# The next batch's scores in float32 ahead of time, q and k in joint tiles, and a softmax in three units of the plan

## The chip, the core and the metric

One core of one Trainium2 chip runs the whole program. The metric is the time on the device of one execution in microseconds, as the median of several. Engines are named as the profile names them: PE is TensorE, PEld its weight loads, DVE is VectorE, ACT is ScalarE, POOL is GpSimd, SP the queue that issues every DMA of this kernel.

## What is computed

For each of four batches with q, k and v of 6080 tokens by 256 channels, attention runs over channels, and a gated two-layer network follows (weights 256 by 2048 and 2048 by 256):

```
qn = q / (norm(q, axis=tokens) + 1e-6);  kn likewise
s  = kn.T @ qn / tau                      # 256 x 256 for each batch
a  = softmax(s, last axis)
x  = v @ a                                # tokens x 256
h  = x @ w_in                             # tokens x 2048
out = (h * sigmoid(1.702 h)) @ w_out      # tokens x 256
```

The weights arrive as float64 and are made float32 on the chip from their 32-bit words.

## The kernel before

**Work.** For each batch the 256 x 256 matrix `a` is folded into `w_in` (`weights`, 12 matmuls of 256 columns for each of 8 `p`), so that the long part goes from v straight to h. The tokens go in six chunks a batch (five of 1024, one of 960). For each chunk and each `p` (two blocks of 128 hidden columns) `unit` makes h with a scheme of seven products in place of eight (L753; each product is three matmuls, high by high, high by low and low by high, in float32r, whose three sums stand for float32), gates it on ACT, splits the result into `gh` and `gl`, and adds 24 matmuls into four output banks (L819). So there are 4 x 6 x 8 = 192 units of 45 matmuls of 512 (or 480) columns.

**Scores.** `s` needs the sum over all tokens of k.T q, and the norms need the sums of squares. The first batch has nothing to hide behind: its 47 tiles of 128 tokens and a tail of 64 are loaded at the start, and each tile's scores are two matmuls in plain float32 (`direct`, L497), into bank `psO0`. For batches 1 to 3, `rows` does it during the batch before, two units of two tiles at a time: load q and k, square them (ACT) and add up (DVE), split both into high and low parts (`qs`, `ks`), six float32r matmuls for each tile (L503) into a `psX` bank, and a DVE addition of that bank into `s_sum`. `finish` then makes norms, softmax and the transposed `a` (`aT_h`, `aT_l`) as one run of steps, in which both exponentials and a first gate (which fetches the gate's table back) are one entry.

**Order.** The program is written out ahead of time by `Plan`: each step has an engine, a modelled cost and a due time; the plan takes, whenever an engine is free, the ready step with the lowest due time, and the engines then run exactly that order. `DUE` holds due times within a unit, in which one unit is 45. Buffers are named slots; a step that uses a slot waits for all users of the slot's previous tenant. SP issues DMAs in the planned order too, and an issue that waits for its buffer holds all issues behind it.

**The first chunk** also converts the weights: in four groups `win_words` and `wout_words` bring words in, `to_float32` (one ACT and six DVE instructions) makes float32 of them, and `win_parts`, `wout_convert` split them. The matmuls on constants of `keep_warm` (8 at the start, 18 after the first scores) compute nothing that is used.

Of the kernel before, what the change touches and what calls it, by code (L numbers as in the profile page):

```python
# [172 lines left out]
def dve_fast(n):  # L173
# [15 lines left out]
def channel_attention_then_glu(  # L189
# [50 lines left out]


# [16 lines left out]
    def load(dst, src, kb, deps=(), uses=(), due=0.0):  # L258
        return g.add("SP", 50 + kb * 2.6, lambda: nc.sync.dma_start(dst(), src), deps, uses, due, lag=2200)
# [34 lines left out]
    def win_words(grp, c, due, slot, after=()):  # L294
        raw = sbuf(slot, [P, GW, 2], U32, "words")
        src = w_in[c * P : (c + 1) * P, 2 * grp * GW : 2 * (grp + 1) * GW].rearrange("p (f w) -> p f w", w=2)
        return raw, load(lambda: raw(), src, 512, after, [raw], due)

    def wout_words(u, due, slot, after=()):
        raw = sbuf(slot, [P, 2, C, 2], U32, "words")  # L300
        src = w_out[2 * u * P : 2 * (u + 1) * P, :].rearrange("(f p) (d w) -> p f d w", p=P, w=2)
        return raw, load(lambda: raw(), src, 512, after, [raw], due)

    def to_float32(out, lows, raw, ready, due, flat):

        n = GW
        lo = sbuf(lows, [P, n], U32, "low")

        def words(i):
            r = raw()  # L310
            return (r.rearrange("p f d w -> p (f d) w") if flat else r)[:, :, i]

        a = g.add(
            "ACT", act(n),
            lambda: nc.scalar.activation(out().bitcast(F32), words(1).bitcast(F32), AF.Abs),
            [ready], [raw, out], due,
# [17 lines left out]
                out().bitcast(U32), in0=words(1), scalar=0xC0000000, in1=out().bitcast(U32),  # L334
# [12 lines left out]
                lo().bitcast(F32), in0=words(0), scalar=2.0**-52, in1=lo().bitcast(F32),  # L347
# [4 lines left out]
        return tt(lambda: out(), lambda: out(), lambda: lo().bitcast(F32), ALU.add, n, [f], [out, lo], due + 6)  # L352

    win_ready = {}

    def win_convert(grp, c, words, due, lows):

        raw, ready = words
        wf = sbuf(f"t{2 * c}", [P, GW], F32, "wf")
        n = to_float32(wf, lows, raw, ready, due, False)  # L360
        store = g.add(
            "SP", 50 + 256 * 2.6,
            lambda: nc.sync.dma_start(win_f[c, :, grp * GW : (grp + 1) * GW], wf()),
            [n], [wf], due + 8, lag=2200,
        )
        win_ready[grp, c] = store
        return wf, n
# [3 lines left out]
    def wout_convert(u, words, due):  # L371
        raw, ready = words
        t = sbuf("t4", [P, GW], F32, "tf")
        n = to_float32(t, "t5", raw, ready, due, True)
        fs = slice(2 * u, 2 * u + 2)
        flat = lambda w: w[:, fs, :].rearrange("p f d -> p (f d)")
        h = cast(lambda: flat(wo_h), lambda: t(), GW, [n], [t], due + 7)
        l = low(lambda: flat(wo_l), lambda: t(), lambda: flat(wo_h), GW, [h], [t], due + 8)
        for f in (2 * u, 2 * u + 1):
            wo_ready[f] = l  # L380
# [3 lines left out]
    class Attention:  # L384
        def __init__(self, b):
            self.b = b
            self.stored = {}
            self.direct = b == 0
            self.units = [(t, min(UT, T - t), P) for t in range(0, T, UT)]
            if TAIL:  # L390
                self.units.append((T, 1, TAIL))
            self.S = bank("psO0", "s") if self.direct else sbuf("sa", [P, NC2 * C], F32, "s_sum")
            self.acc = [sbuf(f"t{6 + i}", [P, UT, C], F32, n) for i, n in enumerate(("acc_q", "acc_k"))]
            self.acc_n = [[], []]
            self.last = None
            self.raw = {}

        def body(self, src):
            return src[self.b, : T * P, :].rearrange("(p t) c -> p t c", p=P)

        def load_direct(self, t0, room, slot, due):

            nt = min(room, T - t0)
            for src, tag in ((q, "q"), (k, "k")):
                t = sbuf(RAW[tag][slot], [P, RT, C], F32, "raw_" + "qk"[tag == "k"])
                cuts = range(nt + 1) if t0 == 0 else (0, nt)
                ns = []
                for a, z in zip(cuts, cuts[1:]):
                    ns.append(load(
                        lambda a=a, z=z, t=t: t()[:, a:z, :], self.body(src)[:, t0 + a : t0 + z, :],  # L410
                        128 * (z - a), (), [t], due,
                    ))
                for o in range(nt):
                    self.raw.setdefault(t0 + o, []).append((t, o, ns[o] if len(ns) > 1 else ns[0]))
                if nt < room and TAIL:
                    n = load(lambda t=t: t()[:TAIL, nt, :], src[self.b, T * P :, :], 64, (), [t], due)
                    self.raw.setdefault(T, []).append((t, nt, n))

        def load_unit(self, u, due, after=()):
            t0, nt, pp = self.units[u]  # L420
            for src, tag in ((q, "raw_q"), (k, "raw_k")):
                t = sbuf(f"t{(u % 2) * 2 + (tag == 'raw_k')}", [P, UT, C], F32, tag)
                if pp == P:
                    n = load(lambda t=t: t()[:, :nt, :], self.body(src)[:, t0 : t0 + nt, :], 128 * nt, after, [t], due)
                else:
                    n = load(lambda t=t: t()[:pp, 0, :], src[self.b, T * P :, :], 64, after, [t], due)
                for o in range(nt):
                    self.raw.setdefault(t0 + o, []).append((t, o, n))

        def rows(self, us, due, after):  # L430

            S = turning("s")
            for i, u in enumerate(us):
                self.unit(u, due + 25 * i, after, S, due + 25 * len(us), i == 0, u == us[-1])
            sa = self.S
            src = lambda: S()[:, : NC2 * C]
            if us[0] == 0:
                self.last = g.add(
                    "DVE", dve(NC2 * C), lambda: nc.vector.tensor_copy(sa(), src()), [self.last], [S, sa],
                    due + 25 * len(us) + 20,  # L440
                )
            else:
                self.last = tt(
                    lambda: sa(), src, lambda: sa(), ALU.add, NC2 * C, [self.last], [S, sa], due + 25 * len(us) + 20,
                )

        def unit(self, u, due, after=(), S=None, pe_due=None, first_=True, last_=True):
            t0, nt, pp = self.units[u]
            S = S or self.S
            if t0 not in self.raw:  # L450
                self.load_unit(u, due - 30, after)
            w = nt * C
            ops = []
            for i, nm in enumerate(("q", "k")):
                buf, o, _ = self.raw[t0][i]
                ready = [self.raw[t0 + j][i][2] for j in range(nt)]
                src = lambda buf=buf, o=o: buf()[:pp, o : o + nt, :]
                acc = self.acc[i]
                if u == 0:
                    self.acc_n[i] = [g.add(  # L460
                        "ACT", act(w), lambda acc=acc, src=src: nc.scalar.activation(acc(), src(), AF.Square),
                        ready, [buf, acc], due + 2,
                    )]
                else:
                    sq = sbuf(f"t{4 + i}", [P, UT, C], F32, "sq")
                    s = g.add(
                        "ACT", act(w),
                        lambda sq=sq, src=src: nc.scalar.activation(sq()[:pp, :nt, :], src(), AF.Square),
                        ready, [buf, sq], due + 4,
                    )  # L470
                    a = lambda acc=acc: acc()[:pp, :nt, :]
                    self.acc_n[i].append(tt(
                        a, a, lambda sq=sq: sq()[:pp, :nt, :], ALU.add, w,
                        [s, self.acc_n[i][-1]], [sq, acc], due + 6,
                    ))
                if self.direct:
                    ops.append((buf, o, ready))
                    continue
# [34 lines left out]
        def finish(self, due):  # L513
# [70 lines left out]
            def fn_ee():  # L584
                for i in range(NC2):
                    fn_e(i)
# [377 lines left out]
```

## Time and profile before

| | |
|---|---|
| median of 3 runs | 2209.85 us (2207.35 to 2214.0) |
| the profiled execution | 2208.2 us, its span 2206.4 us |
| PE busy | 2170.5 us, 98% of the span |
| DVE busy | 1554.9 us, 70% |
| ACT busy | 1336.9 us, 61% |
| mean granted PE clock | 0.994 of full speed |
| moved by DMA | 316.33 MB, mean 143 GB/s |

Busy is time in which an engine has an instruction in work. A PE matmul is pipelined, so the rows' mean for one (about 390 ns) is longer than the step from one to the next. "Idle before" is what an engine stood still ahead of a group, and after the arrow what ended that. The granted clock (PEclk) is a share of 2.4 GHz, with 0.5 as the lower of its two levels.

### The profile page before, as it was taken

Reading aid. Unit: us, or ns where it says so; the run is one execution under the profiler, and the core shown is the slowest. Engines: PE = TensorE matmul, PEld = TensorE weight load, DVE = VectorE, ACT = ScalarE, POOL = GpSimd, SP = SyncE. Lnnn points to the kernel's source line nnn. Section 1 sums busy time; section 2 is a strip of 40 time slices with the busy share of each in tenths; the row PEclk is TensorE's granted clock in tenths of the full one; section 3 lists DMA queues with packets and bytes.
Section 4 is the critical chain, followed back from the end, with each engine's and each line's share of the span. In section 5 each row is a group of like instructions: output and inputs, shape, how many; then the busy total and the mean of one; then the engine's idle time right before and its main releaser. Section 6 shows DMA issues by size and latency. Waiting matters only on the chain.

```text
span 2206.4 us, 27182 instructions
## 1 busy us (share of the span) xinstructions
PE 2170.5 (98%) x10196; PEld 1825.0 (83%) x10196; DVE 1554.9 (70%) x2288; ACT 1336.9 (61%) x2126; POOL 4.9 (0%) x10
## 2 busy tenths in 40 slices
PE   9699999999999999999999999999999999999999
PEld 8578888888888888888888888888888888888887
DVE  7998687776776767766667677776676565565554
ACT  6567666665666666665666666665566555555553
POOL 0000000000000000000000000000000000000000
PEclk9799999999999999999999999999999999999999
DMA  8445344333553433423454343343355332333231
GB/s 293 134 166 189 114 170 160 136 106 122 208 204 115 152 139 141 160 101 121 167 190 179 115 162 134 121 157 118 114 190 191 115 130 103 120 122 113 108 105 49
DMA packets 78163, 316.33 MB, mean 143 GB/s; under 512 B 8400, under 2 KB 10448, under 8 KB 78032
## 3 DMA queue, kind: packets, MB, share of 16 engines
q1 hardware_dynamic: 78032, 314.61, 40.3%
q8 instruction: 80, 1.31, 0.2%
q14 instruction: 51, 0.42, 0.1%
HBM read 258.21 MB, written 56.36 MB: 143 GB/s over the span
## 4 chain that ended last, share of the span: by engine, by line
PE 90%; DVE 4%; DMA 3%; ACT 1%; issue 0%; SPq 0%; ACTq 0%
PE ps_o L819 45%; PE ps_X L753 23%; PE ps_Y L753 11%; PE ps_Z L753 6%; PE ps_s L503 5%; PE ps_w L657 1%; DMA w_ops<-w_op 1%; DMA wf<-win_f 1%; DMA v_raw<-in_vT 1%; DVE gl L273 0%; DVE acc_k L268 0%; DVE h L268 0%; DVE low L346 0%; DVE acc_q L268 0%; DMA raw_k<-in_k 0%
## 5 line engine op out<-in xcount | busy, mean ns | idle before, releaser
L753 PE MATMUL ps_X<-v_op,w_op 128*128 128x512 f32 (+1 forms) x2304 | 637.0, 390 | 12.1 <-ACT s L262 8.4
L819 PE MATMUL ps_o<-gh,wo_h 128*128 128x512 f32 (+1 forms) x1536 | 597.5, 389 | 0.5 <-DVE gh L265 0.5
L819 PE MATMUL ps_o<-gl,wo_h 128*128 128x512 f32 (+1 forms) x1536 | 596.1, 388 | 0.5 <-DVE gl L273 0.5
L819 PE MATMUL ps_o<-gh,wo_l 128*128 128x512 f32 (+1 forms) x1536 | 596.5, 388 | 0.0
L273 DVE TENSOR_TENSOR gl<-h,gh 128x1024 fp32r<-128x1024 f32 (+1 forms) x384 | 466.0, 1214 | 176.9 <-ACT gh L262 156.4
L753 PEld LDWEIGHTS ps_X<-v_op,w_op 128*128 128x128 f32 x2304 | 429.3, 188 | 104.6 <-ACT s L262 12.2
L262 ACT COPY s<-ps_X 128x512 f32<-128x512 f32 (+1 forms) x384 | 222.6, 580 | 314.0 <-PE ps_X L753 260.3
L769 ACT ACTIVATE h<-h 128x512 f32<-128x512 f32 (+3 forms) x384 | 318.8, 839 | 100.3 <-DVE h L268 93.0
L819 PEld LDWEIGHTS ps_o<-gl,wo_h 128*128 128x128 f32 x1536 | 288.5, 188 | 59.1 <-DVE gl L273 1.3
L819 PEld LDWEIGHTS ps_o<-gh,wo_h 128*128 128x128 f32 x1536 | 288.8, 188 | 55.0 <-DVE gh L265 0.9
L819 PEld LDWEIGHTS ps_o<-gh,wo_l 128*128 128x128 f32 x1536 | 288.9, 188 | 53.6
L753 PE MATMUL ps_Y<-v_op,w_op 128*128 128x512 f32 (+1 forms) x1152 | 323.5, 389 | 0.0
L753 PEld LDWEIGHTS ps_Y<-v_op,w_op 128*128 128x128 f32 x1152 | 215.7, 189 | 44.1 <-DVE h L268 1.9
L268 DVE TENSOR_TENSOR h<-ps_Y,s 128x512 f32<-128x512 f32 (+1 forms) x192 | 131.3, 684 | 137.1 <-ACT s L262 135.8
L262 ACT COPY u<-ps_X 128x512 f32<-128x512 f32 (+1 forms) x192 | 111.8, 583 | 187.7 <-PE ps_X L753 180.5
L262 ACT CAST gh<-h 128x1024 fp32r<-128x1024 f32 (+1 forms) x192 | 199.5, 1039 | 17.9 <-PE ps_o L819 13.0
L268 DVE TENSOR_TENSOR h<-ps_Z,s 128x512 f32<-128x512 f32 (+1 forms) x192 | 131.1, 683 | 89.9 <-ACT s L262 80.8
L265 DVE CAST gh<-h 128x1024 fp32r<-128x1024 f32 (+1 forms) x192 | 131.5, 685 | 59.2 <-PE ps_o L819 57.7
L268 DVE TENSOR_TENSOR h<-ps_Y,u 128x512 f32<-128x512 f32 (+1 forms) x192 | 131.4, 684 | 56.7 <-PE ps_Y L753 51.5
L753 PE MATMUL ps_Z<-v_op,w_op 128*128 128x512 f32 (+1 forms) x576 | 162.3, 390 | 0.0
L769 ACT ACTIVATE h<-ps_X 128x512 f32<-128x512 f32 (+1 forms) x192 | 113.8, 593 | 78.9 <-PE ps_X L753 72.3
L753 PEld LDWEIGHTS ps_Z<-v_op,w_op 128*128 128x128 f32 x576 | 109.0, 189 | 22.2
(98 smaller groups left out, 1606.1 us busy)
## 6 DMA issues: line engine op xcount, KB each, us to landing
w_op<-w_ops SPq DMA_DIRECT2D x184, 896.0 KB, 4.6
w_ops<-w_op SPq DMA_DIRECT2D x32, 896.0 KB, 4.6
v_raw<-in_vT SPq DMA_DIRECT2D x20, 1024.0 KB, 7.6
out_T<-osb SPq DMA_DIRECT2D x40, 512.0 KB, 3.2
raw_q<-in_q SPq DMA_DIRECT2D x69, 256.0 KB, 5.2
raw_k<-in_k SPq DMA_DIRECT2D x69, 256.0 KB, 5.3
wf<-win_f SPq DMA_DIRECT2D x24, 256.0 KB, 5.8
raw_q<-in_q SPq DMA_DIRECT2D x11, 512.0 KB, 6.9
```

Source lines behind the costliest of these rows:

```text
L262: return g.add("ACT", act(n, psum), lambda: nc.scalar.copy(dst(), src()), deps, uses, due)
L265: return g.add("DVE", dve_fast(n), lambda: nc.vector.tensor_copy(dst(), src()), deps, uses, due)
L268: return g.add("DVE", dve(n), lambda: nc.vector.tensor_tensor(dst(), a(), b(), op=op), deps, uses, due)
L273: lambda: nc.vector.tensor_tensor(dst(), src(), hi().bitcast(F32), op=ALU.subtract),
L503: nc.tensor.matmul(out, lhsT=rk()[:pp, j, l, ci], rhs=rq()[:pp, j, r, :], start=begin and m == 0, stop=last and m == 2, skip_group_check=True,
L657: nc.tensor.matmul(pb()[:, i * W2 : (i + 1) * W2], lhsT=l()[:, j, ci], rhs=r()[:, j, a * W2 : (a + 1) * W2], start=i == 0 and n == 0, stop ...
L753: nc.tensor.matmul(of(into), lhsT=wt()[:, m, l, :], rhs=v[m]()[:, r, :hw], start=begin and n == 0, stop=True, skip_group_check=True,)
L769: "ACT", act(n, psum), lambda: nc.scalar.activation(dst(), src(), AF.Gelu_apprx_sigmoid),
L819: nc.tensor.matmul(of(ob), lhsT=l[:, f, ds], rhs=rr()[:, n * hw : (n + 1) * hw], start=begin and i == 0 and m == 0, stop=end and i == 1 an ...
```

## The change

- **Joint tiles.** q and k of a unit lie in one tile of two times two times 256 elements; squares, their additions and the high and low splits take 1024 columns in one instruction instead of 512 twice. The weights' conversion takes 1024 columns at a time too, with one words buffer (`os`) and group 0's w_in words in v's buffer (`vr`). The first batch's loads come in units of two tiles through ten buffers, its tail second.
- **Scores ahead (`fill`).** The first 10 units (20 tiles) of the second batch are loaded behind the first batch's, and scored in plain float32 into bank `psO1`; 10 more are loaded and scored in the same way, two units in each of the first five units of the first chunk, through buffers of the next chunk's v. A DVE step (`gather`) adds each bank's sum into `s_sum`: six of them. `rows` later loads these units again for the squares alone and leaves out their splits and matmuls.
- **Softmax in three.** `finish` becomes `norms`, `spread` and `softmax`, with due times of their own; in steady state they belong to three successive units of the loop. Inside `softmax` the two halves of 128 rows go separately: each has its own exponential, reciprocal and transposes. For the first batch all three have the lowest due times. The 18 `keep_warm` matmuls go.
- **Smaller edits.** `between` takes the `psX` bank that the unit before doesn't use, without turning. In the first chunk the second cast to `gh` moves from DVE to ACT. The outputs share one buffer `os`. All due times are set anew, and the plan assumes 3200 ns for a DMA instead of 2200.

The core of the diff:

```diff
 DUE = {
-    "m1": -4, "s1": 5, "m2": 4, "m6": 31, "u2": -17, "c11": 13, "g11": 21, "m5": 35, "u4": 28,
-    "m7": 35, "c22": 5, "m3": 14, "g12": 2, "m4": 42, "c21": 30, "g2": 50, "h1": 60, "l1": 19,
-    "h2": 72, "l2": 37, "o": 137,
+    "m1": 2, "s1": -29, "m2": 6, "m6": 28, "u2": -46, "c11": 11, "g11": 50, "m5": 33, "u4": 20,
+    "m7": 25, "c22": 0, "m3": 9, "g12": 21, "m4": 49, "c21": -6, "g2": 56, "h1": 53, "l1": 53,
+    "h2": 52, "l2": 14, "o": 144, "w0": 54, "w1": 98, "x0": 43, "y0": 110, "x1": 352, "va": -102,
+    "vb": -7, "f0": 55, "fu": -11, "fl": -63, "n": 30, "b": 26, "t": 35,
 }
+LAG = 3200
+GAP = 10
+FILL = (2, 2, 2, 2, 2)
...
+    def between(name):
+        return bank(f"psX{(turns[0] + 1) % 2}", name)
...
+        def scores(self, us, S, due, each=25, direct=False, one=()):
+            prev = None
+            for n_, u in enumerate(us):
+                t0, nt, pp = self.units[u]
...
+                if not direct:
+                    hl = sbuf("hl", [P, 2, UT, 2, C], F32R, "qks")
...
+                            if direct:
+                                nc.tensor.matmul(
+                                    out, lhsT=hl()[:pp, 1, j, ci], rhs=hl()[:pp, 0, j, :],
+                                    start=begin, stop=last, skip_group_check=True,
+                                )
+                                continue
...
+                self.scored.add(u)
+            return prev
...
+        def rows(self, us, due, after):
+            todo = [u for u in us if u not in self.scored]
             for i, u in enumerate(us):
+                self.load_unit(u, due + 25 * i - 30, f"raw{u % 2}", after)
+                self.squares(u, due + 25 * i + 2)
+            if todo:
+                S = between("s")
+                self.gather(S, self.scores(todo, S, due + 25 * len(us)), due + 25 * len(us) + 20)
+
+        def fill(self, us, slots, due, load_due, bank_):
+            for u, slot in zip(us, slots):
+                self.load_unit(u, load_due, slot)
+            self.gather(bank_, self.scores(us, bank_, due, 6, True), due + 6 * len(us))
...
+        def softmax(self, due):
...
+            for i in range(NC2):
...
+                e = g.add("DVE", 1000, fn_s, [*self.factors, self.last], [S, xd, rn, mx], due + 2 * i)
+                e = g.add(
+                    "ACT", 700 if i else 2000,
+                    lambda xi=xi, mi=mi, zi=zi: nc.scalar.activation(xi(), xi(), AF.Exp, bias=mi(), accum_out=zi()),
+                    [e], [xd, mx, zs], due + 2 + 2 * i,
                 )
...
+                z = g.add("DVE", 700, fn_z, [e], [xd, zs], due + 3 + 2 * i)
...
+                ts.append(g.add("PE", 440, fn_t, [z], [xd, pt], due + 4 + 2 * i))
+            g.add("ACT", 1500, lambda: nc.scalar.activation(mx(), mx(), AF.Gelu_apprx_sigmoid), [e], [mx], due + 5)
...
-        r2 = split(h2, [g2], f"2{D % 2}", cast_v)
+        r2 = split(h2, [g2], f"2{D % 2}", cast if D < NU else cast_v)
...
-    at.finish(-120.0)
-    keep_warm(18, [at.last], -118.0)
+    at.norms(-450.0)
+    at.spread(-445.0)
+    at.softmax(-440.0)
+    nf = GAP
+    S = bank("psO1", "s")
+    nxt.fill(range(nf), [RAW[(nu + i) % len(RAW)] for i in range(nf)], DUE["f0"], EARLY + 10 * nu, S)
...
+                W = weights(at, p, parts, due - 45, slot, "wst")
+                fill_us = range(nf, min(nf + (FILL[p] if p < len(FILL) else 0), nu))
+                if fill_us:
+                    fill_bank = between("s")
...
+            if b == 0 and c == 0 and fill_us:
+                slots = [("v01", "v11", "v61")[u % 3] for u in fill_us]
+                nxt.fill(fill_us, slots, due + DUE["fu"], due + DUE["fl"], fill_bank)
+                nf = fill_us.stop
...
                 if s == hi:
-                    nxt.finish(due + 45)
+                    nxt.norms(due + DUE["n"])
+                if s == hi + 1:
+                    nxt.spread(due + DUE["b"])
+                if s == hi + 2:
+                    nxt.softmax(due + DUE["t"])
```

## Rows read from the trace of the kernel before

**Rows 1.** Busy time of each engine by stage, columns in the first line

```profile
core 0: us, PE busy (x) PEld busy (x) DVE busy (x) ACT busy (x) POOL busy (x), PEclk, DMA share, GB/s
0.00:50.50 50.50, 46.77 (x217) 40.99 (x218) 36.02 (x63) 32.80 (x55) 0.70 (x6) 1.00 0.88 320
50.50:76.70 26.20, 11.95 (x70) 10.89 (x69) 24.65 (x59) 12.60 (x25) 1.18 (x1) 0.61 0.13 40
76.70:145.50 68.80, 59.26 (x253) 44.90 (x252) 66.67 (x129) 44.06 (x76) 0.00 (x0) 0.95 0.56 185
145.50:184.00 38.50, 38.48 (x179) 31.86 (x180) 36.70 (x63) 26.79 (x45) 0.00 (x0) 1.00 0.49 184
184.00:600.00 416.00, 415.33 (x2011) 351.05 (x2010) 309.43 (x454) 267.41 (x433) 1.01 (x1) 1.00 0.42 149
```

**Rows 2.** PE's groups, 50.5 to 145.5 us (busy us, mean ns | idle)

```profile
L753 PE MATMUL ps_X<-v_op,w_op 128*128 128x512 f32 x66 | 21.0, 429 | 8.5 <-ACT s L262 7.3 <-ACT u L262 0.7 <-ACT h L769 0.4
L819 PE MATMUL ps_o<-gh,wo_h 128*128 128x512 f32 x30 | 11.8, 395 | 0.5 <-DVE gh L265 0.5
...
L753 PE MATMUL ps_Y<-v_op,w_op 128*128 128x512 f32 x30 | 9.5, 430 | 0.0
L753 PE MATMUL ps_Z<-v_op,w_op 128*128 128x512 f32 x18 | 6.4, 470 | 0.0
L657 PE MATMUL ps_w<-win_h,aT_h 128*128 128x256 f32 x24 | 6.0, 340 | 1.9 <-ACT aT_h L262 1.3 <-ACT w L262 0.7
...
L557 PE MATMUL ps_b<-dq,ones 128*128 128x128 f32 x4 | 1.2, 462 | 4.1 <-DVE dq L549 4.1
```

**Rows 3.** The chain of waits, 0 to 220 us; start us, us, what

```profile
149.90 1.43 PE ps_w L657 x12
...
165.14 0.68 PE ps_X L753 x3
...
202.28 1.43 PE ps_s L503 x12
```

**Rows 4.** Groups of instructions, whole execution

```profile
L503 PE MATMUL ps_s<-qs,ks 128*128 128x256 f32 (+1 forms) x864 | 121.0, 283 | 0.0
...
L497 PE MATMUL ps_s<-raw_q,raw_k 128*128 128x256 f32 (+1 forms) x192 | 42.2, 381 | 2.7 <-DMA raw_k<-in_k 2.7
```

**Rows 5.** The stage view for tile ps_s alone

```profile
9.30:50.50 41.20, 40.15 (x184) 34.85 (x184) 0.00 (x0) 1.00 0.93 348
```

**Rows 6.** PE's waits, 0 to 160 us (total, times, longest)

```profile
PE ps_t L604 <- DVE x L595: 8.2, 1, 8.2
PE ps_X L753 <- ACT s L262: 7.3, 5, 2.5
...
PE ps_s L497 <- DMA raw_k<-in_k: 2.7, 1, 2.7
```

**Rows 7.** VectorE's groups in 50.5 to 145.5 us

```profile
L273 DVE TENSOR_TENSOR gl<-h,gh 128x1024 fp32r<-128x1024 f32 x9 | 11.0, 1224 | 0.1
...
L333 DVE SCALAR_TENSOR_TENSOR wf<-words,wf 128x512 uint32<-128x512 uint32 x6 | 4.1, 688 | 0.1
...
L265 DVE CAST gh<-h 128x1024 fp32r<-128x1024 f32 x4 | 2.7, 684 | 0.0
L325 DVE TENSOR_SCALAR wf<-wf 128x512 uint32<-128x512 uint32 x6 | 2.6, 427 | 0.2
```

**Rows 8.** Instructions in order of time around the first softmax

```profile
62.47 0.42 DVE L320 TENSOR_SCALAR tf<-tf 128x512 f32<-128x512 f32 x1
63.21 1.28 ACT L587 ACT_TABLE_LOAD   x1
64.50 0.20 ACT L587 ACTIVATE mx<-mx 128x2 f32<-128x2 f32 x1
...
76.69 1.48 PE L753 MATMUL ps_X<-v_op,w_op 128*128 128x512 f32 x3
```

**Rows 9.** Line of the softmax's exponentials (ns min/median/max, first and last start)

```profile
L575 ACT ACT_TABLE_LOAD  x3: 1283/1283/1283, 488.7 to 1561.3; - x3
```

More of the change, by code (lines that the diff above doesn't have):

```diff
@@ L398, in body @@
[L398 to L408, printed above, removed]
+                self.units.insert(1 if b == 0 else len(self.units), (T, 1, TAIL))
@@ new lines, in __init__, with load_unit @@
+            self.S = self.acc = self.acc_n = self.last = None
+            self.raw = {}
+            self.scored = set()
+        def load_unit(self, u, due, slot, after=(), by_tile=False):
+            t0, nt, pp = self.units[u]
+            t = sbuf(slot, [P, 2, UT, C], F32, "raw_qk")
+            ns = []
+            for o in range(nt) if by_tile else (slice(0, nt),):
+                o = o if isinstance(o, slice) else slice(o, o + 1)
+                for i, src in enumerate((q, k)):
+                    if pp == P:
+                        part = src[self.b, : T * P, :].rearrange("(p t) c -> p t c", p=P)[:, t0 + o.start : t0 + o.stop, :]
+                    else:
+                        part = src[self.b, T * P :, :].rearrange("p (t c) -> p t c", t=1)
@@ L419, in load_unit @@
-        def load_unit(self, u, due, after=()):
-            t0, nt, pp = self.units[u]
[L421 to L428, printed above, removed]
+                        lambda t=t, i=i, o=o: t()[:pp, i, o, :], part, 128 * (o.stop - o.start), after, [t], due,
+                    ))
@@ L430, in rows, with gather @@
+        def gather(self, S, n, due):
+            src = lambda: S()[:, : NC2 * C]
+            if self.S is None:
+                sa = self.S = sbuf("sa", [P, NC2 * C], F32, "s_sum")
+                fn = lambda: nc.vector.tensor_copy(sa(), src())
+            else:
+                sa = self.S
+                fn = lambda: nc.vector.tensor_tensor(sa(), src(), sa(), op=ALU.add)
+            self.last = g.add("DVE", dve(NC2 * C), fn, [n, self.last], [S, sa], due)
         def rows(self, us, due, after):
-            S = turning("s")
+            todo = [u for u in us if u not in self.scored]
@@ L433, in rows @@
             for i, u in enumerate(us):
[L434 to L445, printed above, removed]
@@ new lines, in rows, with norms @@
+                self.squares(u, due + 25 * i + 2)
[6 more added lines that the diff above has]
+            self.gather(bank_, self.scores(us, bank_, due, 6, True), due + 6 * len(us))
+        def norms(self, due):
+            self.xd = xd = sbuf("acc", [P, 2, NC2, C], F32, "x_dq")
+            self.rn = rn = small("rn", 2 * NC2)
+            diag = lambda: xd()[:, 1, 0, :].rearrange("p (i x) -> p i x", i=NC2)
+            pn = between("n")
+            acc = self.acc
+            half_ = lambda t: acc()[:, :, t, :]
+            sums = tt(lambda: half_(0), lambda: half_(0), lambda: half_(1), ALU.add, 2 * C, [self.acc_n], [acc], due)
@@ L549, in fn_b, with spread @@
                     nc.vector.tensor_scalar_mul(diag()[:, i, :], ident, rn()[:, i : i + 1])
-                nc.vector.tensor_scalar_mul(rn()[:, NC2:], rn()[:, NC2:], rtau)
-            a = g.add("DVE", 1200, fn_b, [a, const_i, tau_n], [rn, dq], due + 4)
-            pb = turning("b")
+            self.rn_n = g.add("DVE", 800, fn_b, [a, const_i], [rn, xd], due + 4)
+        def spread(self, due):
+            xd, rn = self.xd, self.rn
+            diag = lambda: xd()[:, 1, 0, :].rearrange("p (i x) -> p i x", i=NC2)
+            self.rqb = lambda: xd()[:, 1, 1, :]
+            pb = between("b")
             def fn_c():
@@ L589, in finish @@
-            e = g.add("ACT", 4200, fn_ee, e, [x, mx, zs], due + 9)
-            def fn_z():
-                nc.vector.tensor_scalar_add(zs(), zs(), 1e-9)
-                nc.vector.reciprocal(zs(), zs())
-                for i in range(NC2):
-                    nc.vector.tensor_scalar_mul(x()[:, i, :], x()[:, i, :], zs()[:, i : i + 1])
-            e = g.add("DVE", 1300, fn_z, [e], [x, zs], due + 10)
-            pt = turning("t")
-            ptv = lambda: pt().rearrange("p (c x) -> p c x", c=NC2)
@@ L601, in fn_t @@
-            def fn_t():
-                for j in range(NC2):
-                    for i in range(NC2):
+            c = g.add("PE", 440, fn_c, [self.rn_n], [pb, xd], due)
+            a = g.add(
+                "DVE", 200, lambda: nc.vector.tensor_scalar_mul(rn()[:, NC2:], rn()[:, NC2:], rtau), [self.rn_n, tau_n], [rn],
+                due,
+            )
+            c = g.add("DVE", 430, lambda: nc.vector.tensor_copy(self.rqb(), pb()[:, :C]), [c], [pb, xd], due + 1)
+            self.factors = [a, c]
@@ L618, in win_parts @@
-        for c in range(NC2):
-            if wf is None:
-                b = sbuf(("t0", "t2")[c], [P, GW], F32, "wf")
-                n = load(
-                    lambda b=b: b(), win_f[c, :, grp * GW : (grp + 1) * GW], 256,
-                    [win_ready[grp, c], *after], [b], due - 25,
-                )
-            else:
-                b, n = wf[c]
-            halves.append((b, n))
-        wi_h = sbuf("f0", [P, NC2, GW], F32R, "win_h")
-        wi_l = sbuf("f1", [P, NC2, GW], F32R, "win_l")
@@ L630, in win_parts @@
-        got = []
-        for c, (b, n) in enumerate(halves):
-            h = cast(lambda c=c: wi_h()[:, c, :], lambda b=b: b(), GW, [n], [b, wi_h], due + c)
-            got.append(low(
-                lambda c=c: wi_l()[:, c, :], lambda b=b: b(), lambda c=c: wi_h()[:, c, :], GW,
-                [h], [b, wi_h, wi_l], due + 2 + c,
-            ))
-        return wi_h, wi_l, got
+        if wf is None:
+            t = sbuf("raw0", [P, NC2 * GW], F32, "wf")
+            wf = t, load(lambda: by_c(t), columns(grp), 512, [win_ready[grp], *after], [t], due - 25)
@@ L642, in channel_attention_then_glu, with weights @@
+        t, n = wf
+        wi = sbuf("hl", [P, 2, NC2 * GW], F32R, "win")
+        h = cast(lambda: wi()[:, 0], lambda: t(), NC2 * GW, [n], [t, wi], due)
+        l = low(lambda: wi()[:, 1], lambda: t(), lambda: wi()[:, 0], NC2 * GW, [h], [t, wi], due + 2)
+        return wi, [h, l]
     P1, P2, P4, P3, P5, P7, P6 = range(NK)
-    def weights(at, p, parts_, due, slot):
-        wi_h, wi_l, got = parts_
+    def weights(at, p, parts_, due, slot, sums):
+        wi, got = parts_
+        aT = at.aT
@@ L647, in weights @@
         a = p % PAIRS
         W2 = 2 * P
-        pb = turning("w")
+        pb = between("w")
         def fn():
@@ new lines, in channel_attention_then_glu @@
+    for u in range(nu):
+        at.squares(u, EARLY + 10 * u + 10, ("sq", "wst")[u % 2])
+    at.S = bank("psO0", "s")
+    at.last = at.scores(range(nu), at.S, EARLY + 10, 10, True)
+    wf = win_convert(0, words, EARLY + DUE["x0"], "gl20")
+    parts = win_parts(0, EARLY + DUE["y0"], wf)
+    last_load = at.raw[nu - 1][1][-1]
+    wout_convert(0, words_o, EARLY + DUE["x1"], "sq", "gl21")
+    V = {(0, 0): values(0, 0, 0, DUE["va"], DUE["vb"], [last_load])}
+    at.norms(-450.0)
+    at.spread(-445.0)
@@ L917, in channel_attention_then_glu @@
             if b + 1 < B:
-                if s == lo:
+                if s == 0 and b > 0:
                     nxt = Attention(b + 1)
-                while nxt is not None and done < len(segs) and s >= lo + done * (hi - lo) / len(segs):
+                while s >= lo and done < len(segs) and s >= lo + done * (hi - lo) / len(segs):
                     nxt.rows(segs[done], due + 40, here)
@@ L929, in channel_attention_then_glu @@
                         nparts = win_parts(n // PAIRS, due + 20, after=here)
-                    weights(nxt, n, nparts, due + 60, "wst")
-        if nxt is not None:
-            at = nxt
+                    weights(nxt, n, nparts, due + 60, "wst", "sa")
+        at = nxt
     with tc.manual_schedule():
```

337 lines of the change are left out of this document (137 added, 200 removed).

## The prediction, made before the changed kernel ran

> **What bounds the kernel now.** I read the stage view first [rows 1], because an average over 2206 us hides the start. Its columns to look at are PE's busy time against the length of the stretch, and the clock. From 145.5 us on PE is never idle to speak of: 38.48 of 38.5 us, then 415.33 of 416. There every matmul that is left out shortens the run by its own step, and nothing else does. Before 145.5 us it is different. Until 50.5 us PE works on the first batch's scores, nearly without a pause from 9.3 us on [rows 5], with the DMA engines 0.88 busy beside it. From 50.5 to 76.7 us PE mostly waits for the softmax, and its granted clock falls to a mean of 0.61, so part of it runs at 1.2 GHz. From 76.7 to 145.5 us, most of the first chunk, PE looks 59.26 of 68.8 us busy, while DVE is busy 66.67: there DVE, which converts weights and splits h, sets the pace.
>
> Busy time flatters PE, since a lone matmul counts with its whole latency. So I count work instead. A step from one group of three matmuls to the next is 0.68 us in the saturated part, 0.227 us a matmul; twelve of 256 columns take 1.43 us, 0.119 us each [rows 3]. Between 50.5 and 145.5 us PE did 66 + 30 + 18 products' matmuls and three groups of 30 for the outputs, 204 x 0.227 = 46.2 us, and three groups of 24 for the folded weights (only the first of each three is shown), 72 x 0.119 = 8.6 us [rows 2]. That is 54.8 of 95.0 us, so **40.2 us of PE time are lost there**, plus 2.7 us before 9.3 us in which PE waited for k [rows 6]: 42.9 us in all. In the first chunk alone, from 76.7 us, it is 68.8 less the 46.2 and 48 x 0.119 = 5.7, which is 16.9 us.
>
> **What the change removes from the saturated part.** Forty tiles of six float32r matmuls no longer run there. Twelve of them step in 1.43 us [rows 3], so a tile is 0.715 us and forty are **28.6 us**. These 240 are a subset of the 864 shown [rows 4], the rest stays. The splits and bank additions that go with them were on ACT and DVE, busy 267 and 309 of 416 us [rows 1]: worth nothing while PE is full. The second loading of the 20 units, 10.5 MB, goes where the DMA engines are 0.13 to 0.56 busy; hidden too, and if it were not, 10.5 MB at the 320 GB/s of the first stage would be 33 us.
>
> **What it adds.** The same tiles in float32: 192 rows of matmuls make 48 tiles, so four rows a tile [rows 4]; 184 rows took 40.15 us [rows 5], which is 0.873 us a tile and **34.9 us** for forty. So PE's total work rises by 6.3 us. The change can only gain by placing this work into the 42.9 us that PE loses now.
>
> **The softmax gap.** The first 20 tiles, 17.5 us, follow the first batch's scores on PE. Their loads go through buffers that those scores set free one by one, 512 KB for every two tiles, or 1.75 us of PE: 300 GB/s, under the 320 that the first stage moved. So they should stream on as before. The softmax itself gets shorter. Before, a weight-conversion step stood on DVE between the exponentials and the reciprocal [rows 8], and the transposes waited 8.2 us [rows 6]; with the lowest due times and the sums of squares mostly done before the scores end, the chain should need 8 to 12 us instead of the 26 from the stage's start to the first product at 76.69 us. But the first unit's h buffers are those of the fill, so it can't get far before the fill's tiles are read. I expect PE to stay busy from about 50 to 68 us and at full clock.
>
> **The first chunk.** The other 20 tiles, 17.5 us, go into a stretch in which PE lost 16.9 us. Each group of four tiles shares its `psX` bank with that unit's products, so it must be loaded, scored and gathered by DVE before the unit's first product. Its loads join the one SP queue, where an issue that waits for its buffer holds the weights' words and the w_ops stores behind it; a late words load would stop DVE's conversion and with it the next group's products. DVE is the other half of the account. It was busy 24.65 + 66.67 = 91.3 of the 95 us. The second `gh` cast moves to ACT: four at 0.684 us, 2.7 us less. Conversions at 1024 columns: two fast ones of 0.427 us become one like the 0.684 us cast, two slow ones of 0.688 us become one like the 1.224 us subtraction [rows 7]; with three of each a pair saves 3 x 0.17 + 3 x 0.152 = 0.97 us, and the stretch has about 6.5 pairs, 6.3 us less. Six gathers of 512 columns at 0.688 us add 4.1 us. DVE's net is 4.9 us less. So DVE would bring the same units through in about 90 us, and PE needs 54.8 + 34.9 plus some 2 us for the norms, the spread and the transposes, 91.7 us. The two engines are nearly level, and two level engines that hand work to each other don't both run full. Of the 16.9 us I keep 5 as still lost; zero and 16.9 are the bounds.
>
> **The steady part.** Softmax in three costs PE nothing more, but both exponentials were one entry and now gates of other units can come between them. A table load is 1283 ns [rows 9], and before, one followed the pair [rows 8]. Two more for each of three later softmaxes are 6 x 1.283 = 7.7 us on ACT, which idles a third of the time: I take 0, with 0 and 7.7 as bounds. The new due times reorder all 192 units; I take no change.
>
> Rows 8 show a table load at 63.21 us and the next ACT instruction at 64.50, right at its end. The Trainium skill (ScalarE: Activation LUTs, What ACT_TABLE_LOAD costs) counts a drain of about 1380 ns on top, 2.66 us for each switch; by that the six would be 16 us, by the row 7.7. The trace shows no such drain here.
>
> **The sum.** Gain = 28.6 + 42.9 - 34.9 - L = 36.6 - L, where L is what PE still loses before it is full: 2 us of small steps and 5 us in the chunk, L = 7. So 29.6 us; put plainly, the first 145 us take about as long as now and do 35 us more work. From the profiled execution's 2208.2 us that gives 2178.6. The median of the runs stands 1.65 us above that execution, which would make 2180.3; I say 2179.
>
> **Rivals.**
> *The chunk stays at DVE's pace and the fill comes on top.* The bank shared by fill and products, and DVE's 97% in this stretch, speak for it; DVE's 4.9 us less and the lowest priority of the words speak against. Then L = 2 + 16.9 and the gain is 17.7: 2190.5 us. Chance 0.17.
> *The exponentials' tables.* All six extra loads reach PE through late snaps: 29.6 - 7.7 = 21.9, so 2186.3 us. For it: PE waits now and then for ACT's snaps. Against: PE has the output products of older units to go on with. Chance 0.06. The Trainium skill's page named above says to do all exponentials together, which speaks against this edit.
> *The float32 scores are not hidden at all.* The fill's loads come late, and the softmax gap and the chunk stay as they are, with 34.9 us in front of them: 28.6 - 34.9, a loss of 6.3, 2214.5 us, within 0.3%. Against it: the buffers come free long before. Chance 0.03.
> *Slower: late snaps in every unit.* The new due times put the first product later and the gates later, and the X bank's chain (product, snap, product) is the tightest of a unit. In the ramp such a wait for a snap was 7.3 / 5 = 1.46 us [rows 6]. If one unit in five of the 192 waited so, it would be 56 us, a loss of 27: 2235 us; it turns slower from a little over one in ten (28 us). The saturated rows show no such wait now, and the snaps get earlier due times. Chance 0.05.
>
> **How the numbers follow.** My forecast, L between 0 and about 14, 2171.6 to 2185.6 us, has 0.69. The range to 2193 takes in most of the first two rivals: 2170 to 2193 leaves out about 0.15. A difference of 0.3%, 6.6 us, is about what a measurement here can tell from none. Faster by more than that: 0.69 + 0.17 + 0.06 = 0.92; within it 0.03; slower 0.05.
>
> **What the profile after would show.** If right: 240 fewer float32r score matmuls and 160 more rows of float32 ones; PE's clock at full speed from 50 to 77 us; PE full from about the same time as now, with its first product well before 76.69 us; DVE's share in the chunk still over nine tenths. It would be wrong if PE shows waits for the fill's loads or for a gather in the first 180 us (first rival), or idle time before `ps_X` beyond 200 us (tables, snaps); and lower than 2171 us only if the saturated part itself steps faster than 0.227 us a matmul.

## The result and the profile after

The changed kernel takes **2178.9 us** (2178.29 to 2180.95, four runs) where the one before takes 2209.37 on the same chip: a ratio of 0.9861, 95% interval 0.9844 to 0.9878. In a second set of runs it was 2178.51 against 2207.39 us, 0.9869 (0.9855 to 0.9882). The forecast was 2179 in 2170 to 2193. The profiled execution took 2179.19 us, its span 2177.4, which is 29.0 us less than the span before.

The stages of the changed kernel, cut at the same times as [rows 1] and with the same columns:

```profile
0.00:50.50 50.50, 45.26 (x196) 37.90 (x197) 35.99 (x35) 29.51 (x29) 0.70 (x6) 1.00 0.95 341
50.50:76.70 26.20, 26.20 (x141) 23.47 (x140) 23.06 (x48) 12.27 (x24) 1.45 (x1) 1.00 0.78 299
76.70:145.50 68.80, 64.40 (x300) 53.40 (x299) 61.76 (x95) 41.14 (x62) 0.00 (x0) 0.98 0.55 194
145.50:184.00 38.50, 38.50 (x182) 32.36 (x182) 32.33 (x50) 28.24 (x44) 0.00 (x0) 1.00 0.49 169
184.00:600.00 416.00, 416.00 (x1921) 349.34 (x1921) 297.77 (x412) 265.41 (x395) 1.01 (x1) 1.00 0.46 164
```

PE is now busy without a gap from 50.5 to 76.7 us, at the full clock where it had 0.61 before. In the chunk it is busy 64.40 of 68.8 us, and from 145.5 us on it doesn't wait at all.

PE's groups between 50.5 and 145.5 us, as [rows 2]:

```profile
L467 PE MATMUL ps_s<-raw_qk 128*128 128x256 f32 x174 | 39.6, 380 | 0.0
L741 PE MATMUL ps_X<-v_op,w_op 128*128 128x512 f32 x60 | 18.6, 422 | 4.4 <-ACT s L270 2.8 <-DVE s_sum L494 1.6
L807 PE MATMUL ps_o<-gh,wo_h 128*128 128x512 f32 x25 | 10.1, 406 | 0.0
...
L645 PE MATMUL ps_w<-win,aT 128*128 128x256 f32 x72 | 9.6, 285 | 0.0
L741 PE MATMUL ps_Y<-v_op,w_op 128*128 128x512 f32 x27 | 7.7, 393 | 0.0
L741 PE MATMUL ps_Z<-v_op,w_op 128*128 128x512 f32 x15 | 5.2, 461 | 0.0
L526 PE MATMUL ps_n<-ones,acc 128*128 128x1 f32 x8 | 0.9, 240 | 0.0
L601 PE MATMUL ps_t<-ident,x_dq 128*128 128x128 f32 x4 | 0.8, 273 | 0.0
L552 PE MATMUL ps_b<-x_dq,ones 128*128 128x128 f32 x4 | 0.6, 275 | 0.0
```

Counted as in the prediction: 102 product matmuls and 3 x 25 for the outputs at 0.227 us are 40.1 us, 72 for the weights 8.6 (they stand in one group now), 174 rows of float32 scores at 0.218 us 38.0: 86.7 of 95 us. **The stretch loses 8.3 us where it lost 40.2.** Of these the norms, the transposes and the spread are 2.3 us (the last three lines). The price is that the chunk is 6 us of products and outputs behind the old one at 145.5 us.

What PE waited for in the first 160 us, as [rows 6]:

```profile
PE ps_s L467 <- DMA raw_qk<-in_k: 4.2, 6, 1.3
PE ps_X L741 <- ACT s L270: 2.8, 2, 2.1
PE ps_X L741 <- DVE s_sum L494: 1.6, 1, 1.6
```

The 2.7 us of waiting for k at the start did not go away; they became 4.2, in six waits between 10 and 32 us.

From the groups of the whole execution, the scores as in [rows 4] and all of ACT's table loads:

```profile
L473 PE MATMUL ps_s<-qks 128*128 128x256 f32 (+1 forms) x624 | 85.9, 283 | 0.0
...
L467 PE MATMUL ps_s<-raw_qk 128*128 128x256 f32 x352 | 81.0, 385 | 4.2 <-DMA raw_qk<-in_k 4.2
...
L588 ACT ACT_TABLE_LOAD x3 | 3.8, 1283 | 0.1
...
L607 ACT ACT_TABLE_LOAD x2 | 2.6, 1283 | 0.0
L757 ACT ACT_TABLE_LOAD x2 | 2.6, 1283 | 0.0
...
L429 ACT ACT_TABLE_LOAD x1 | 1.3, 1283 | 4.9 <-DMA raw_qk<-in_k 4.9
```

624 rows of float32r scores instead of 864, 352 of float32 instead of 192: exactly the 240 less and 160 more of the prediction. The table loads are eight, and the kernel before had eight too: four for the gates, three for the exponentials, one at the start.

### The profile page after: what moved, and what is told of

It is laid out like the page before. It is cut to its first block, busy times and chain, and to the rows that moved or that the text cites. A ratio compares the mean times of both kernels' runs of the same rounds, so it can differ in the third digit from the quotient of the medians.

```text
span 2177.4 us, 26297 instructions
## 1 busy us (share of the span) xinstructions
PE 2162.9 (99%) x10080; PEld 1820.8 (84%) x10080; DVE 1507.0 (69%) x2021; ACT 1307.8 (60%) x1911; POOL 5.9 (0%) x10
## 4 chain that ended last, share of the span: by engine, by line
PE 97%; DMA 1%; DVE 1%; ACT 0%; SPq 0%; issue 0%; ACTq 0%
PE ps_o L807 48%; PE ps_X L741 24%; PE ps_Y L741 12%; PE ps_Z L741 6%; PE ps_s L473 3%; PE ps_s L467 2%; PE ps_w L645 2%; DMA words<-in_w_in 0%; DMA words<-in_w_out 0%; DMA raw_qk<-in_k 0%; SPq L267 0%; DMA raw_qk<-in_q 0%; ACT wf L327 0%; PE ps_n L526 0%; DVE wf L344 0%; DVE low L357 0%
## 5 line engine op out<-in xcount | busy, mean ns | idle before, releaser
L757 ACT ACTIVATE h<-h 128x1024 f32<-128x1024 f32 (+3 forms) x384 | 319.4, 839 | 59.8 <-DVE h L276 51.8
L270 ACT CAST gh<-h 128x1024 fp32r<-128x1024 f32 (+1 forms) x200 | 207.9, 1040 | 9.0 <-PE ps_o L807 2.6
L273 DVE CAST gh<-h 128x1024 fp32r<-128x1024 f32 (+1 forms) x184 | 126.4, 687 | 106.6 <-PE ps_o L807 97.2
L276 DVE TENSOR_TENSOR acc<-acc,sq 128x1024 f32<-128x1024 f32 (+2 forms) x96 | 113.0, 1177 | 27.1 <-ACT sq L434 24.8
```

The source lines that it names most:

```text
L270: return g.add("ACT", act(n, psum), lambda: nc.scalar.copy(dst(), src()), deps, uses, due)
L273: return g.add("DVE", dve_fast(n), lambda: nc.vector.tensor_copy(dst(), src()), deps, uses, due)
L276: return g.add("DVE", dve(n), lambda: nc.vector.tensor_tensor(dst(), a(), b(), op=op), deps, uses, due)
L757: "ACT", act(n, psum), lambda: nc.scalar.activation(dst(), src(), AF.Gelu_apprx_sigmoid),
```

## The experiments

All ratios are to the kernel before on the same chip; a thousandth is 2.2 us. The intervals are 0.0009 to 0.0017 to either side, mostly from the kernel before, whose runs spread over 3 to 7 us; the runs of one of these kernels lie within 0.6 to 3.8 us. So differences between them of 3 us are read. Smaller ones are read only between kernels timed on the same chip whose runs don't overlap, and are otherwise called none.

**No fill.** `GAP = 10` and `FILL` are set to nothing; all else as changed.

```diff
-GAP = 10
-FILL = (2, 2, 2, 2, 2)
+GAP = 0
+FILL = ()
...
```

> The changed kernel without the fill (all 48 tiles of the second batch's scores go through the float32r way later). Packing theory (the gain is work moved out of the full part of PE into time that PE lost): 28.6 us return to the full part and 34.9 us leave the start, of which most turns into idle time again: about 11 us in the softmax gap and some 8 us in the first chunk instead of 4. So 2179 + 28.6 - 34.9 + 11 + 8 = about 2192 us (2186 to 2200), PE's first product near 68 us. Rival 1 (the other edits alone make the gain, the fill pays for itself at most): 2176 to 2181. Rival 2 (the fill alone makes the gain): 2205 to 2212.

2197.98 us, ratio 0.9957 (0.9942 to 0.9972). Both rivals fall: the other edits give 0.4%, the fill the rest. Its stages (columns as in [rows 1]) and PE's longest waits in the first 184 us:

```profile
50.50:76.70 26.20, 13.36 (x60) 10.29 (x59) 24.53 (x50) 13.02 (x25) 1.39 (x1) 0.73 0.22 78
76.70:145.50 68.80, 61.59 (x277) 49.85 (x278) 64.50 (x96) 46.88 (x70) 0.00 (x0) 0.93 0.50 181
```

```profile
PE ps_t L601 <- DVE zs L593: 5.4, 1, 5.4
...
PE ps_X L741 <- DVE v_op L281: 4.0, 1, 4.0
PE ps_o L807 <- DVE gl L281: 2.4, 1, 2.4
```

PE's gap is there again, 12.8 us idle between 50.5 and 76.7 and a clock of 0.73. The expectation named 2192 and was 6 us too low. In the chunk PE waits for DVE's steps (`v_op` 4.0 us, `gl` 2.4), where the kernel before waited for ACT's `s` (7.3 us [rows 6]), and its granted clock falls there too, to 0.93; the run on the clock below gives some 3 of the 6 us back.

**Half of the fill each.** The gap's part only, then the chunk's part only:

```diff
-FILL = (2, 2, 2, 2, 2)
+FILL = ()
...
-GAP = 10
+GAP = 0
```

> The changed kernel with only the 10 units of the softmax gap filled ahead. Packing theory: 14.3 us of the 28.6 are saved, 17.5 us of float32 work cover some 11 us of gap: about 8 us under the kernel without fill, near 2184 us (2180 to 2190). If the gap's part is worth nothing, it equals the kernel without fill.

> The changed kernel with only the five groups of two units in the first chunk filled ahead. Packing theory: 14.3 us saved, 17.5 us added in a chunk that then has some 8 to 12 us of idle PE: 5 to 9 us under the kernel without fill, near 2186 us (2182 to 2192). If DVE's pace takes the fill on top (the first rival of the prediction), it is 3 us or more above the kernel without fill.

The gap's ten units: 2182.72 us, 0.9889 (0.9873 to 0.9906), 15 us under no fill. The chunk's ten units: 2190.43 us, 0.9924 (0.9909 to 0.9938), 7.3 us under it. The second stage of each, first the gap's, then the chunk's:

```profile
50.50:76.70 26.20, 26.20 (x141) 23.18 (x139) 24.58 (x51) 12.46 (x25) 1.45 (x1) 1.00 0.63 240
```

```profile
50.50:76.70 26.20, 16.75 (x78) 14.35 (x78) 22.25 (x47) 12.78 (x24) 1.45 (x1) 0.74 0.24 73
```

With the gap's fill PE has no idle time in that stage; with the chunk's alone 9.5 us stay. So the gap's half brought as much as the 14.3 us that it removes later, though it puts 17.5 us of float32 work into the start. The chunk's half cost about 7 of its 14.3. The two halves don't add up: 15 and 7 us alone, 19 together, since the chunk's half brings only 4 to 5 us on top of the gap's. Its rival, a fill that lies on top of DVE's pace, would have made that kernel slower than no fill, and falls.

**The clock alone.** No fill, but 72 matmuls on constants in PE's idle places, with the order of the other steps nearly unchanged (in the traces, 69 of PE's 10144 other matmul records stand in another place):

```diff
+    for i in range(18):
+        keep_warm(4, [at.last], DUE["f0"] + i)
```

> The kernel without fill, with 72 idle-time matmuls on constants that nothing uses, placed by the plan with low priority so that PE's clock stays up through the softmax gap. If the gap's fill gains by the work it places there, only the clock's part comes back: the 24 weight matmuls took 5.2 us at the lower clock against 3.2 at full speed, so 2 to 4 us under the kernel without fill (a ratio of 0.994). Rival (the fill gains mainly because it keeps the clock up): 10 us or more under it (0.991 or less). If the clock is of no account: equal (0.9957).

2194.61 us, 0.9942 (0.993 to 0.9955): 3.3 us under no fill. Its second stage:

```profile
50.50:76.70 26.20, 24.90 (x175) 21.78 (x175) 25.04 (x51) 13.56 (x26) 1.40 (x1) 1.00 0.23 79
```

The clock is 1.00 through the gap, and in the chunk as well (0.93 without these matmuls), and still 12 us more are to be had by the gap's fill. The fill gains by the work it places, and some 3 of its 15 us by the clock. So of the 14.3 us that it removes about 12 remain, and its float32 work costs some 2.

**The due times within a unit.** The changed kernel with the 21 values of the kernel before:

```diff
 DUE = {
-    "m1": 2, "s1": -29, "m2": 6, "m6": 28, "u2": -46, "c11": 11, "g11": 50, "m5": 33, "u4": 20,
+    "m1": -4, "s1": 5, "m2": 4, "m6": 31, "u2": -17, "c11": 13, "g11": 21, "m5": 35, "u4": 28,
...
```

> The changed kernel with the 21 due times within a unit of the kernel before. Packing theory: the order inside a unit matters little, 2179 to 2186 us; the full part may show a few us of waits for snaps again, as the kernel before did (3.6 us from 184 to 2100 us). Rival (the new due times carry much of the gain): 2190 us or more, with waits ahead of the X bank's products in many units.

2184.0 us, 0.9897 (0.9882 to 0.9911), about 6 us more than the changed kernel: inside the range that the first theory gave, but not little. PE's waits from 184 us to the end of this kernel; the changed one has none there:

```profile
PE ps_X L741 <- ACT u L270: 3.1, 3, 1.3
PE ps_X L741 <- DVE aT L281: 1.0, 1, 1.0
PE ps_X L741 <- ACT s L270: 0.3, 1, 0.3
```

4.4 us of the six are here, late snaps above all (a snap is ACT's copy of a product's bank, `s` or `u`); the rest lies before.

The same edit in the kernel without fill:

> The kernel without fill and with the 21 due times within a unit of the kernel before: what is left of the change is the joint tiles, the softmax in three, the cast on ACT and the other due times. If the due times add on their own (5 us, as with the fill): a ratio of 0.998 to the kernel before, 3 to 5 us faster than it. If they only pay together with the fill: 0.9957, as without fill.

2205.13 us, 0.9989 (0.998 to 0.9998). So the due times give 7 us without the fill as well, and joint tiles, split softmax, the cast on ACT and the other due times together about 2.4 (by the interval 0.4 to 4.4). These were not taken apart.

**More fill.** All of the batch's units, beside the changed kernel unaltered:

```diff
-FILL = (2, 2, 2, 2, 2)
+FILL = (3, 3, 3, 3, 3)
```

> The changed kernel unaltered, as the yardstick on this chip for the three beside it: a ratio of 0.986 to the kernel before, 2176 to 2181 us.

> The changed kernel with all 25 units scored ahead (three units in each of the first five of the first chunk instead of two): 5 units, 8 whole tiles and the tail, more. Packing theory: 6.4 us or so leave the full part, 7.9 us of float32 work come into a chunk in which PE is idle for only 4.4 us between 80 and 96 us; so nothing is left to gain: 2177 to 2183 us, a ratio of 0.985 to 0.988. Rival (the chunk still has room that the busy time hides, or only the full part's work counts): 6 us less, 2173 us or under, 0.983.

The changed kernel: 2178.51 us, 0.9869 (0.9855 to 0.9882). All units: 2179.07 us, 0.9870 (0.9855 to 0.9885): nothing gained. The chunk has no room left for more work on PE.

**Does PE or DVE set the pace of the start?** Three runs: the first w_out words 13 units of loading later; the chunk's fill one unit later; and the second cast to `gh` back on DVE.

```diff
-    "h2": 52, "l2": 14, "o": 144, "w0": 54, "w1": 98, "x0": 43, "y0": 110, "x1": 352, "va": -102,
+    "h2": 52, "l2": 14, "o": 144, "w0": 54, "w1": 230, "x0": 43, "y0": 110, "x1": 352, "va": -102,
...
-FILL = (2, 2, 2, 2, 2)
+FILL = (0, 2, 2, 2, 2, 2)
...
-        r2 = split(h2, [g2], f"2{D % 2}", cast if D < NU else cast_v)
+        r2 = split(h2, [g2], f"2{D % 2}", cast_v)
```

> The changed kernel with the first w_out words due 13 units of loading later, so that 1 MB leaves the stretch from 10 to 31 us in which PE now waits 4.2 us for q and k with the DMA engines fully busy. If those waits are DMA's bandwidth and PE's scores set the end of that stage: 2 to 3 us less than the changed kernel beside it. If DVE's squares set it (its additions end at 50.5 us as well), or the words come too late for DVE: equal or up to 3 us more.

> The changed kernel with the chunk's five groups of fill one unit later (units 1 to 5 instead of 0 to 4), so that the first unit's products no longer share their bank with a group of fill. In the changed kernel PE waits there for the gather and then for a snap, 4.5 us in all between 80 and 92 us. If the shared bank is the cause and PE sets the pace of the start: 2 to 4 us less than the changed kernel (ratio 0.985). If DVE sets the pace of the first chunk, PE's earlier start is given back later in it: within 1 us (0.9865 to 0.9875).

> The changed kernel with the second cast to gh of the first chunk's units back on DVE, 8 casts of 0.684 us or 5.5 us of DVE work more. If DVE sets the pace of the first chunk: 2 to 5 us more than the changed kernel (ratio 0.988 to 0.989). If PE sets it: within 1 us of it (0.987).

*Words later:* 2180.41 us, 0.9878 (0.9864 to 0.9891), about 2 us more than the changed kernel on the same chip, whose runs all lie under this one's. The first stage and the stretch from 82 to 97 us of the changed kernel's second run, then of this one:

```profile
0.00:50.50 50.50, 45.01 (x198) 37.93 (x199) 35.87 (x35) 29.49 (x29) 0.70 (x6) 1.00 0.95 343
...
82.00:97.00 15.00, 9.50 (x44) 6.47 (x43) 11.55 (x15) 6.52 (x10) 0.00 (x0) 1.00 0.64 239
```

```profile
0.00:50.50 50.50, 46.79 (x217) 40.45 (x218) 36.63 (x36) 30.08 (x29) 0.70 (x6) 1.00 0.96 348
...
82.00:97.00 15.00, 10.81 (x26) 6.64 (x27) 10.57 (x14) 6.36 (x9) 0.00 (x0) 0.66 0.60 225
```

By 50.5 us PE is 19 instructions ahead (217 against 198), some 4 us, and its wait for q and k is 2.6 us instead of 4.4. So the words' bandwidth did cause waits at the start. What was won there is lost again between 82 and 97 us: PE comes to its first X product earlier, waits 3.0 us for the gather ahead of it instead of 1.6, and then its granted clock is down to a mean of 0.66 where it was 1.00. The same 24 matmuls of the products, up to the next matmul for the weights, take 13.9 us (82.96 to 96.85) instead of 10.6 (84.71 to 95.33). That the words come later hardly shows as a wait: between 76.7 and 145.5 us ACT waits 6.6 us for w_out's words, and 6.3 in the changed kernel.

*Fill one unit later:* 2178.1 us, 0.9868 (0.9855 to 0.9881), the same. PE's three longest waits in its first 184 us:

```profile
PE ps_s L467 <- DMA raw_qk<-in_k: 4.1, 4, 1.3
PE ps_X L741 <- ACT s L270: 1.5, 2, 0.7
PE ps_s L467 <- ACT w L270: 1.3, 1, 1.3
```

The wait for the gather is gone, that for the snap is halved, a new one for a copy of the weights (the third row) has come, with others for DVE, 5.2 us in all after the loads against 5.5 in the changed kernel's second run, and the end has not moved. ACT's wait for w_out's words, 6.2 us in the changed kernel between 50.5 and 145.5 us, is 0.5 here: those late words don't set the end either.

*The cast on DVE:* 2184.29 us, 0.9893 (0.9879 to 0.9906). 5.5 us more work on DVE made the kernel 5.3 us longer, give or take 3. The fourth stage shows where:

```profile
145.50:184.00 38.50, 35.47 (x160) 29.00 (x159) 34.79 (x55) 25.25 (x40) 0.00 (x0) 0.96 0.56 188
```

PE now idles 3 us there, after 145.5 us, where the changed kernel has none, and its clock falls to 0.96. So DVE has next to no slack in the chunk. It does not set the pace alone, though. In the changed kernel PE is full while DVE is busy 92% of the time:

```profile
100.00:145.50 45.50, 45.50 (x221) 38.83 (x220) 41.94 (x64) 30.70 (x47) 0.00 (x0) 1.00 0.49 171
```

The two are level.

**Less work for DVE.** The last addition of each weight conversion goes to POOL:

```diff
-        return out, tt(lambda: out(), lambda: out(), lambda: lo().bitcast(F32), ALU.add, n, [f], [out, lo], due + 6)
+        return out, g.add(
+            "POOL", 2400,
+            lambda: nc.gpsimd.tensor_tensor(out(), out(), lo().bitcast(F32), op=ALU.add), [f], [out, lo], due + 6,
+        )
```

> The changed kernel with the last step of each weight conversion, the addition of 1024 columns, on POOL instead of DVE: eight steps of 1.22 us, six of them after 50 us, 7.3 us off DVE. If DVE's pace is all that is left in the first chunk: 2 to 5 us less than the changed kernel (ratio 0.985 or less; PE has about 6 us of waits there to give back). If POOL's step is so long that the weights come later, or PE is now as full as its order of work allows: within 1 us (0.9865 to 0.9875) or more than the changed kernel.

2182.07 us, 0.9886 (0.9869 to 0.9902), some 4 us longer: a miss for the hope. In order of time, around one of POOL's steps:

```profile
111.96 2.36 POOL L365 TENSOR_TENSOR wf<-wf,low 128x1024 f32<-128x1024 f32 x1 [15.49 <-issue]
...
112.55 1.92 DVE L276 TENSOR_TENSOR sx<-w 128x128 f32<-128x128 f32 x1
...
114.51 0.29 DVE L276 TENSOR_TENSOR sx<-sx,w 128x128 f32<-128x128 f32 x1
```

The `sx` addition of DVE, 0.28 us otherwise, takes 1.92 and ends with POOL's step (114.47 and 114.32 us). Two of DVE's groups between 50.5 and 145.5 us, here and then in the changed kernel:

```profile
L276 DVE TENSOR_TENSOR sx<-w 128x128 f32<-128x128 f32 x12 | 8.1, 694 | 0.0
```

```profile
L276 DVE TENSOR_TENSOR sx<-w 128x128 f32<-128x128 f32 x12 | 3.2, 284 | 1.2 <-ACT w L270 1.2
```

In this stretch five DVE instructions are stretched in that way, by 9.0 us together, where 7.3 us of work were taken off. So DVE did not get the time back, and this run does not test what less work on DVE would bring. How the 4 us divide between this and POOL's longer step (2.4 us against 1.22) was not separated.

## Why the prediction was right, point by point

**The full part.** 28.6 us for 240 matmuls: their count is as said, and the gap's half alone brought 15 us, 12 of them without the clock's part, where 14.3 were to leave the full part. Confirmed.

**The float32 work.** 160 rows at 0.218 us, 34.9 us. Confirmed by count and rate.

**The gap.** The loads streamed on as expected and PE stayed full at 1.00 of the clock. But the softmax was not as short as 8 to 12 us. In the changed kernel's order of time:

```profile
53.60 0.15 DVE L532 COPY rn<-ps_n 128x4 f32<-128x4 f32 x1
...
54.45 1.23 DVE L357 SCALAR_TENSOR_TENSOR low<-words,low 128x1024 f32<-128x1024 uint32 x1
...
55.59 0.16 DVE L536 TENSOR_SCALAR rn<-rn 128x4 f32<-128x4 f32 x1
...
74.12 1.04 PE L741 MATMUL ps_Z<-v_op,w_op 128*128 128x512 f32 x3
75.00 0.85 PE L741 MATMUL ps_Y<-v_op,w_op 128*128 128x512 f32 x3
...
85.22 1.65 PE L741 MATMUL ps_X<-v_op,w_op 128*128 128x512 f32 x6 [1.60 <-DVE s_sum L494]
```

A weight conversion (the 1.23 us step) still stands between the norms' steps on DVE, though its due times are later than theirs. The folded weights start at 67.8 us; without fill the first product stood at 69.5, 19 us after the stage's start. That was of no account with the fill, which covered it. The sign I named, a first product well before 76.69 us, came only for `ps_Z` and `ps_Y` (74.12 and 75.00), and no more than 2.6 us before; the X chain starts at 85.22, behind the first group of fill.

**The loss L.** Predicted 7 = 2 small steps + 5 in the chunk, none at the start. Measured 2.3 + 6.0 + 4.2 at the start. So L is 12.5, and by the formula the gain would be 36.6 - 12.5 = 24.1. The term that failed most is the recovery of the 2.7 us before 9.3 us: PE still waits for the first batch's q and k, while w_out's words share the DMA engines with them (2.6 us with these words later). The fill is not the cause: without it the wait is 4.5 us.

**The due times.** I took no change; here the prediction was mis-sized the other way. The last output matmul of the first batch, before and after:

```profile
650.16 0.38 PE L819 MATMUL ps_o<-gl,wo_h 128*128 128x480 f32 x1
```

```profile
626.66 0.38 PE L807 MATMUL ps_o<-gl,wo_h 128*128 128x480 f32 x1
```

That is 23.5 us earlier, near the 24.1 of the formula. After it no matmul is left out, and yet the last output matmuls of the three later batches come 25.8, 28.2 and 29.1 us earlier: 5.6 us more that the sum doesn't have. With the old due times 4.4 of the 5.6 are gone again, most of them waits: the kernel before had 3.4 us of PE waits after 145.5 us, and the changed one has none. With the old due times and no fill, 1.0 remains for the other edits. So the total came out within a microsecond by luck: a loss 5.5 us larger than forecast, and 5.6 us of steady gain that was put at nothing, cancel.

**DVE level with PE in the chunk.** Borne out: more fill gains nothing, PE's early starts are given back, and DVE's 5.5 us come through one for one. DVE's share was 61.76 of 68.8, 0.898, just under the nine tenths I named; over the 95 us it was busy 84.8, 6.5 less than before, where I had 4.9. PE is full from about 95 us, sooner than the 145.5 I expected.

**The rivals.** The fill on top of DVE's pace: refuted by the chunk's half. Its sign, a wait for a gather, did show, once and for 1.6 us (at 85.22 us above): the bank shared by fill and products costs that, not the rival's 16.9. PE never waited for the fill's own loads. Float32 scores not hidden: refuted by the gap. Late snaps in every unit: none after 184 us; the reverse is true. The tables: no more loads than before. At the second softmax only a copy stood between the exponentials, and a gate never did, so no switch was added. A table load and its neighbours on ACT there:

```profile
464.37 0.59 ACT L270 COPY u<-ps_X 128x512 f32<-128x512 f32 x1 [1.38 <-PE ps_X L741]
464.97 1.28 ACT L588 ACT_TABLE_LOAD   x1
466.27 0.51 ACT L588 ACTIVATE x_dq<-x_dq,mx 128x256 f32<-128x256 f32 x1
```

The copy before ends at 464.96 us and the exponential starts at the load's end (466.25 us), so of the drain that the Trainium skill adds (ScalarE: Activation LUTs, What ACT_TABLE_LOAD costs) nothing shows here either.

## What to carry to other kernels

Count the work of the engine that sets the end, not its busy time: 98% busy hid 40 us in the first 145. Work that costs more in itself (0.873 us a tile against 0.715) can still gain when it fills idle time and empties the full part. But such a place has a second engine beside it: once both are level, as DVE and PE here, more filling and earlier starts come back as waits. Whether less work on the second engine would help was not shown: moved to POOL, it came back as longer DVE instructions.

## What the runs showed of the hardware

A DVE addition with two operands in SBUF that ran beside POOL's addition of 1024 columns took 1.92 us instead of 0.28 and ended 0.15 us after it, while an addition that read PSUM just before took its usual 0.68. Beside seven of the eight such POOL steps one DVE instruction was stretched, to between 1.90 and 3.20 us; beside the eighth (at 94.06 us) only additions that read PSUM ran, and they took 0.68 to 0.69. Who starts first seems to matter: twice a DVE instruction of 1024 columns with two operands in SBUF began just before POOL's step (0.17 and 0.01 us, at 23.06 and 139.93 us) and took its usual 1.22 us, and those two POOL steps took 3.26 and 3.47 us instead of 2.4. The Trainium skill (GPSIMD Engine Reference, Key points) says that POOL shares its SBUF interfaces with VectorE and that DVE instructions with two SBUF inputs, among others, contend with it; this run agrees.
